# Attention prologue of a fused attention and two-MLP kernel, written in a fixed order

## The chip, the cores and the metric

The kernel runs on one core of a Trainium2 chip. The metric is the device time in microseconds (us). The five engines are called by the names of the profile: PE (TensorE), DVE (VectorE), ACT (ScalarE), POOL (GpSimd) and SP (SyncE, which issues the DMAs here).

## What is computed

```python
def _attn_ref(q, k, v):                      # 8 batches, 8 heads, 576 tokens, 64 wide
    k_p = k.reshape(B, H, Sp, pool, D).mean(axis=3)      # pool = 8, Sp = 72
    v_p = v.reshape(B, H, Sp, pool, D).mean(axis=3)
    scores = scale * np.matmul(q, k_p.transpose(0, 1, 3, 2))
    scores = scores - np.max(scores, axis=-1, keepdims=True)
    attn = np.exp(scores)
    attn = attn / (np.sum(attn, axis=-1, keepdims=True) + 1e-09)
    return np.matmul(attn, v_p)
...
x = attn_out.transpose(0, 2, 1, 3).reshape(4608, 512)
h = x @ w_in;  x = (h - np.tanh(h)) @ w_out      # first MLP, 512 -> 2048 -> 512
h = x @ w_in2; out = (h * np.cos(h)) @ w_out2    # second MLP, the same sizes
```

## The kernel before

The 4608 tokens are cut into nine blocks of 512. A block goes through 16 steps f, one for each 128 of the 2048 hidden columns. In a step PE forms `h` with twelve 512-wide matmuls (`emit_h`, L553: four chunks of x, each as high part times high weight, low part times high weight, high part times low weight), ACT and DVE form h - tanh(h) (`g1_act`, `g1_rest`, `g_second`), and two steps later PE adds the product with `w_out` to four accumulators (`emit_out1`, L590). The second MLP follows for all blocks.

Attention runs beside the first MLP. A batch's K and V are pooled in chunks of 128 pooled rows (`pool_kv`): for batch 0 by one `tensor_reduce` on DVE (L266), for later batches by three additions on POOL (L269 twice, L270). K's sums are copied side by side (L272, ACT), transposed (`kprep`, L302) and put into a block-diagonal tile `bd` by ACT. A Q tile is loaded (`load_q`, SP's queue), transposed (`s1`, L332), multiplied with `bd` in two halves (`s2`, L346; row maximum and subtraction on DVE, L349 and L353; exponential on ACT, L355), normalised (`norm`, L360 to L364), transposed again (`s3`, L375 and L385; copies `ah` and `ar`), and multiplied with V (`pv`, L406; `place_v` puts V's sums into `vbd` and `vbr`). The result is x as a high part `xh` (ACT, L409) and a low part `xl` (DVE, L413). Batch 0 has five tiles: 0 to 3 fill block 0's 512 tokens in two groups of two, tile 4 holds the last 64.

The weights of the first MLP are split into high and low parts in 32 pieces, piece n for step n // 2, w_in before w_out (`converter`): ACT's Prelu into a buffer `cva` (L157), two DVE passes (L166, L168), ACT's copy to the high part (L172), POOL's subtraction to the low part (L162 or L149), one of two buffers held from the first to the last. Pieces for even f stay resident (`wi`, `wo`), those for odd f lie in a ring (`ri`, `ro`).

What stands from L795 to L873 is the prologue: loads, batch 0's attention and the first conversions in program order, which a scheduler turns into an order for each engine; it may also move instructions of block 0 ahead. The steps of block 0 then take attention work of later batches from a list `items`, and conversions by `w1_tick`. Each engine runs its own instructions in its order and waits for the others by semaphores.

Of the kernel before, what the change touches and what calls it, by code (L numbers as in the profile page):

```python
# [8 lines left out]
F32 = mybir.dt.float32  # L9
# [11 lines left out]
T = 0.25  # L21
# [17 lines left out]
def fused_kernel(ctx: ExitStack, tc: tile.TileContext, q, k, v, w1i, w1o, w2i, w2o, out):  # L39
# [98 lines left out]
    def converter(pieces, raws, dest, loaded, done, allowed):  # L138
        prev = None
        a = None  # L140
        for n in range(len(pieces) + 1):
            if n < len(pieces):
# [12 lines left out]
                a = ap.tile([128, 512], F32, tag="cva", name="cva", bufs=2)  # L155
# [99 lines left out]
    def pool_kv(which, b, c):  # L255
# [9 lines left out]
        if b == 0:  # L265
# [5 lines left out]
        if which == "k" and c == NKC - 1:  # L271
            nc.scalar.activation(out=kp[:, :, D:2 * D], in_=kp[:, :, 0:D], func=AF.Copy)  # L272
# [47 lines left out]
    def load_q(t, pool=None, tag="qt", bufs=2):  # L320
        n = t["n"]
        qt = (pool or ap).tile([128, H * D], F32, tag=tag, name="qt", bufs=bufs)
        nc.sync.dma_start(
            out=qt[:n].rearrange("p (h d) -> p h d", h=H),
            in_=q[t["b"], :, t["s"]:t["s"] + n, :].rearrange("h s d -> s h d"))
        t["qt"] = qt
# [9 lines left out]

    def s2(t, half):
        n = t["n"]
        if half == 0:
            t["e"] = eb[t["i"] % 2]  # L340
# [25 lines left out]
    def s3(t, part):  # L366
        n, e, g, o = t["n"], t["e"], t["g"], t["o"]
        if o == 0 and part == 0:
            g["ah"] = ap.tile([128, NP, 320], F32R, tag="ah", name="ah")
            g["al"] = ap.tile([128, NP, 320], F32R, tag="al", name="al")  # L370
            g["ar"] = ap.tile([3 * GR, NG, 320], F32R, tag="ar", name="ar")
        at = att_tile()
        if part == 0:
# [4 lines left out]
            al = g["al"][:, :, o:o + n]  # L378
            if t["b"] in PV32:
                nc.scalar.activation(out=ah.bitcast(F32), in_=av, func=AF.Copy)  # L380
                return None
            nc.scalar.activation(out=ah, in_=av, func=AF.Copy)
# [71 lines left out]
    item(lambda: kprep(0))  # L454
# [206 lines left out]
    w1_conv = converter(w1_pieces, w1_raw, w1_dest, w1_loaded, w1_fin, w1_allowed)  # L661
# [131 lines left out]
    if True:  # L793

        for c in range(3):  # L795
            load_k(0, c)
        load_k(0, 3, cp, "t0", 2)
        load_k(0, 4, cp, "t0", 2)
        load_q(tiles[0])
        w1_load(0)  # L800
        w1_load(1)
        load_q(tiles[1])
        make_identity(nc, ident)
        nc.vector.memset(bias_q, SQ_B)
        nc.vector.memset(bias_m, -T * T)
        nc.vector.memset(bias_r, MAGIC)
        nc.vector.memset(bias_c, HALF_PI)
        nc.gpsimd.memset(kp, 0.0)
        nc.gpsimd.memset(bd, 0.0)
        values()  # L810
        for c, (tag, bufs) in enumerate((("t4", 2), ("t4", 2), ("gh", 3), ("gh", 3), ("gh", 3), ("t2", 1))):
            load_v(0, c, cp, tag, bufs)
        load_q(tiles[2], cp, "xe", 4)
        load_q(tiles[3], cp, "xe", 4)
        load_q(tiles[4], cp, "xe", 4)
        for n in range(2, 6):
            w1_load(n)

# [4 lines left out]
        banks.extend([None, acc[0], "h", acc[1], None, acc[2], "h", acc[3]])  # L823
        for c in range(NKC):
            pool_kv("k", 0, c)
        s1(tiles[0])
        kprep(0)
        kprep(1)
        for c in range(NP + NG):
            pool_kv("v", 0, c)  # L830
        for j, (c0, c1) in enumerate(((0, SP), (SP, 128), (0, SP - RR), (SP - RR, 128))):
            nc.vector.tensor_reduce(mk[:, j:j + 1], ident[:, c0:c1], axis=AX.X, op=ALU.add)
        nc.vector.tensor_reduce(
            mk[:, 4:6], ident.rearrange("p (c g i) -> p g c i", g=2, i=RR), axis=AX.XY, op=ALU.add)
        nc.vector.tensor_scalar(mk, mk, 1.0 / POOL, None, op0=ALU.mult)
        place_v(0)
        for c in range(3):
            load_k(1, c)
        s1(tiles[1])
        l0 = s2(tiles[0], 0)  # L840
        l1 = s2(tiles[0], 1)
        done(l0)
        done(l1)
        w1_tick(2)
        for j in range(n0):
            t = tiles[j]
            if j + 1 < n1:
                l0 = s2(tiles[j + 1], 0)
# [142 lines left out]
```

## Time and profile before

| | us |
|---|---|
| median of three runs | 1785.73 (1785.09 to 1785.97) |
| the profiled execution | 1787.28 |
| its span, first to last instruction | 1785.5 |
| PE busy | 1737.2 |
| first matmul of `h`, block 0 | 59.2 |

The page gives busy time by engine over the whole span. The table by stage gives the same for chosen stretches, with PE's granted clock as a share of 2.4 GHz. The chain of waits follows the work that ended last back to what released it, in order of time. A timeline row begins with its start, in us from the span's start, and ends with the idle time ahead of it and what ended that. A group of instructions is given with its mean duration in ns.

### The profile page before, as it was taken

Reading aid. Unit: us, or ns where it says so; the run is one execution under the profiler, and the core shown is the slowest. Engines: PE = TensorE matmul, PEld = TensorE weight load, DVE = VectorE, ACT = ScalarE, POOL = GpSimd, SP = SyncE. Lnnn points to the kernel's source line nnn. Section 1 sums busy time; section 2 is a strip of 40 time slices with the busy share of each in tenths; the row PEclk is TensorE's granted clock in tenths of the full one; section 3 lists DMA queues with packets and bytes.
Section 4 is the critical chain, followed back from the end, with each engine's and each line's share of the span. In section 5 each row is a group of like instructions: output and inputs, shape, how many; then the busy total and the mean of one; then the engine's idle time right before and its main releaser. Section 6 shows DMA issues by size and latency. Waiting matters only on the chain.

```text
span 1785.5 us, 22632 instructions
## 1 busy us (share of the span) xinstructions
PE 1737.2 (97%) x7960; PEld 1426.6 (80%) x7960; DVE 1244.2 (70%) x2109; ACT 1158.1 (65%) x2079; POOL 279.2 (16%) x342
## 2 busy tenths in 40 slices
PE   5989999999999999999999999999999999999999
PEld 3666878888888888888888888888888888888887
DVE  8699778778888887776666566565656666566655
ACT  4576767767677776766665666666666666666665
POOL 3764244213424141100000000000000000000000
PEclk8799999999999999999999999999999999999999
DMA  7565655645655554523277401010101010101000
GB/s 234 162 215 192 211 161 182 212 159 185 205 177 184 188 197 142 175 100 109 83 262 254 154 0 48 1 48 1 48 1 47 1 47 1 48 1 48 1 24 24
DMA packets 116402, 202.29 MB, mean 113 GB/s; under 512 B 45376, under 2 KB 61760, under 8 KB 116288
## 3 DMA queue, kind: packets, MB, share of 16 engines
q1 hardware_dynamic: 116288, 200.84, 33.9%
q8 instruction: 63, 1.03, 0.2%
q14 instruction: 51, 0.42, 0.1%
HBM read 156.76 MB, written 44.04 MB: 112 GB/s over the span
## 4 chain that ended last, share of the span: by engine, by line
PE 86%; DVE 5%; DMA 3%; ACT 2%; POOL 2%; issue 1%; SPq 0%; POOLq 0%; DVEq 0%; ACTq 0%
PE h L751 22%; PE acc L779 21%; PE h L553 19%; PE acc L590 18%; PE att L406 2%; PE att L346 2%; DMA kv<-in_k_dram 1%; POOL kv L269 1%; PE att L375 1%; DVE cva L168 1%; DMA raw<-in_moe_w_in_dram 1%; DVE gl L583 1%; DVE w L576 1%; PE att L332 1%; DVE w L575 1%
## 5 line engine op out<-in xcount | busy, mean ns | idle before, releaser
L751 PE MATMUL h<-xh,wi 128*128 128x512 f32 x1008 | 330.8, 389 | 0.0
L779 PE MATMUL acc<-wo,gh 128*128 128x512 f32 x1008 | 310.3, 389 | 0.0
L762 DVE SCALAR_TENSOR_TENSOR r<-kk,h 128x512 f32<-128x512 f32 (+1 forms) x145 | 99.1, 684 | 182.2 <-ACT kk L760 181.8
L751 PEld LDWEIGHTS h<-xh,wi 128*128 128x128 f32 x1008 | 189.3, 188 | 39.4
L779 PEld LDWEIGHTS acc<-wo,gh 128*128 128x128 f32 x1008 | 189.2, 188 | 39.3
L770 ACT ACTIVATE r<-r 128x512 f32<-128x512 f32 (+1 forms) x145 | 91.3, 630 | 195.2 <-DVE r L764 195.2
L553 PE MATMUL h<-xh,wi 128*128 128x512 f32 x576 | 199.8, 407 | 1.2 <-POOL wi L162 0.6
L553 PE MATMUL h<-xh,ri 128*128 128x512 f32 x576 | 196.2, 400 | 0.0
L571 DVE SCALAR_TENSOR_TENSOR w<-u,h 128x512 f32<-128x512 f32 x144 | 98.2, 682 | 140.6 <-ACT th L565 140.5
L751 PE MATMUL h<-xl,wi 128*128 128x512 f32 x504 | 196.1, 389 | 0.0
L779 PE MATMUL acc<-wo,gl 128*128 128x512 f32 x504 | 196.1, 389 | 0.0
L772 DVE TENSOR_TENSOR co<-co,h 128x512 f32<-128x512 f32 (+1 forms) x145 | 99.1, 684 | 117.6 <-ACT co L771 117.6
L590 PE MATMUL acc<-gh,wo 128*128 128x512 f32 x576 | 178.9, 392 | 0.0
L590 PE MATMUL acc<-gh,ro 128*128 128x512 f32 x576 | 177.4, 389 | 0.0
L759 ACT ACTIVATE kk<-h,bias_r 128x512 f32<-128x512 f32 (+1 forms) x145 | 99.6, 687 | 91.6 <-PE h L751 91.6
L564 ACT ACTIVATE u<-h 128x512 f32<-128x512 f32 x144 | 85.6, 594 | 91.6 <-PE h L553 91.1
L582 ACT ACTIVATE gh<-w 128x512 fp32r<-128x512 f32 x144 | 90.9, 631 | 66.3 <-DVE w L576 65.2
L583 DVE TENSOR_TENSOR gl<-w,gh 128x512 fp32r<-128x512 f32 x144 | 109.7, 762 | 28.2 <-ACT gh L582 26.0
L553 PEld LDWEIGHTS h<-xh,wi 128*128 128x128 f32 x576 | 109.7, 191 | 24.4 <-POOL wi L162 1.1
L590 PEld LDWEIGHTS acc<-gh,wo 128*128 128x128 f32 x576 | 109.1, 190 | 22.9
L576 DVE COPY_PREDICATED w<-u,th 128x512 f32<-128x512 uint32 x144 | 113.3, 787 | 19.1 <-ACT u L574 6.1
L590 PEld LDWEIGHTS acc<-gh,ro 128*128 128x128 f32 x576 | 108.1, 188 | 22.5
(165 smaller groups left out, 3530.4 us busy)
## 6 DMA issues: line engine op xcount, KB each, us to landing
ri<-s1i SPq DMA_DIRECT2D x64, 512.0 KB, 3.5
ro<-s1o SPq DMA_DIRECT2D x64, 512.0 KB, 3.4
raw<-in_moe_w_in_dram SPq DMA_DIRECT2D x32, 512.0 KB, 3.9
raw<-in_moe_w_out_dram SPq DMA_DIRECT2D x32, 512.0 KB, 4.0
x1s<-xe SPq DMA_DIRECT2D x36, 256.0 KB, 4.7
xr<-x1s SPq DMA_DIRECT2D x36, 256.0 KB, 3.9
out_dram<-xe SPq DMA_DIRECT2D x36, 256.0 KB, 2.1
kv<-in_k_dram SPq DMA_DIRECT2D x32, 256.0 KB, 3.9
```

The costliest lines, as they stand in the source:

```text
L553: nc.tensor.matmul(out=h[:, off:off + m], lhsT=wi[:, c, wsel, :], rhs=xt[:, r:r + m], start=(n == 0), stop=(n == 3 * KC - 1))
L571: nc.vector.scalar_tensor_tensor(w, u, C2, h, op0=ALU.mult, op1=ALU.mult)
L576: step_end[0] = nc.vector.copy_predicated(w, u.bitcast(U32), th)
L582: nc.scalar.activation(out=gh[:, a:e], in_=w[:, a:e], func=AF.Copy)
L583: nc.vector.tensor_tensor(gl[:, a:e], w[:, a:e], gh[:, a:e].bitcast(F32), op=ALU.subtract)
L590: nc.tensor.matmul(out=acc[d], lhsT=wo[:, wsel, d * 128:(d + 1) * 128], rhs=gt, start=(f == 0 and n == 0), stop=(f == NF - 1 and n == 2))
L751: nc.tensor.matmul(out=h, lhsT=wi[:, c, wsel, :], rhs=xt[:, o:o + BLK], start=(n == 0), stop=(n == 3 * KC - 1))
L759: nc.scalar.activation(out=kk[:, a:e], in_=h[:, a:e], func=AF.Identity, bias=bias_r, scale=INV_2PI)
L762: nc.vector.scalar_tensor_tensor(r[:, a:e], kk[:, a:e], -PI2_HI, h[:, a:e], op0=ALU.mult, op1=ALU.add)
L770: nc.scalar.activation(out=r[:, a:e], in_=r[:, a:e], func=AF.Abs)
L772: nc.vector.tensor_tensor(co[:, a:e], co[:, a:e], h[:, a:e], op=ALU.mult)
L779: nc.tensor.matmul(out=acc[t], lhsT=gt[:, t * 128:(t + 1) * 128], rhs=wo[:, wsel, :], start=(f == 0 and n == 0), stop=(f == NF - 1 and n = ...
```

## The change

The prologue is written under `manual_schedule`, which keeps the order of its instructions; the scheduler can still place others between them. In it:
- A one-element exponential comes first on ACT, and with it the table load.
- Q tiles 0 to 3 are loaded from ACT's queue, tile 4 is left to `items`.
- Batch 0's K is copied and transposed in two parts, as its chunks come; its V is summed on POOL.
- The conversion has four buffers instead of two: `wide`, which has the place of `al` (batches 0 and 1 don't use `al`), holds two more.
- Tiles 2 and 3 have score buffers of their own, in the place of resident weights that come later.
- `spin(n)` puts n transposes of the identity into PE's order, 38 in all, into an accumulator that nobody reads.
- The pooling of the next batch's K, tile 4's scores and exponentials move to `items`, and of the conversions 8 calls of `w1_tick` stay where up to 26 were.

```diff
-                a = ap.tile([128, 512], F32, tag="cva", name="cva", bufs=2)
+                a = own[n % len(own)] if own else ap.tile([128, 512], F32, tag="cva", name="cva", bufs=2)
...
-        if b == 0:
+        if b == 0 and which == "k":
             nc.vector.tensor_reduce(o, t[:n].rearrange("p (r d) -> p d r", r=POOL), axis=AX.X, op=ALU.add)
         else:
...
-        if which == "k" and c == NKC - 1:
-            nc.scalar.activation(out=kp[:, :, D:2 * D], in_=kp[:, :, 0:D], func=AF.Copy)
+        if which == "k" and (c == NKC - 1 or (b == 0 and c == KSPLIT[0][1] - 1)):
+            c0 = (KSPLIT[1][0] if c == NKC - 1 else 0) if b == 0 else 0
+            nc.scalar.activation(out=kp[:, c0:c + 1, D:2 * D], in_=kp[:, c0:c + 1, 0:D], func=AF.Copy)
...
     t = tiles[n0]
-    item(lambda: kprep(0))
+    item(lambda t=t: s1(t), lambda t=t: load_q(t))
+    post_kv("k", 1, 0)
+    item(lambda t=t: s2(t, 0), apart=True)
+    post_kv("k", 1, 1)
+    item(lambda t=t: s2(t, 1))
+    post_kv("k", 1, 2)
...
+    post_kv("k", 1, 4)
+    item(lambda: kprep(0), apart=True)
     post(lambda t=t: norm(t))
...
+        with tc.manual_schedule():
+            warm = cp.tile([128, 1], F32, name="warm")
...
+            nc.scalar.activation(out=warm, in_=bias_m, func=AF.Exp)
+            make_identity(nc, ident)
+            for c in range(3):
+                load_k(0, c)
+            load_k(0, 3, cp, "t0", 2)
+            load_k(0, 4, cp, "t0", 2)
+            load_q(tiles[0], queue=nc.scalar)
+            load_q(tiles[1], queue=nc.scalar)
+            w1_load(0)
+            for c, (tag, bufs) in enumerate((("t4", 2), ("t4", 2), ("gh", 3), ("gh", 3), ("gh", 3), ("t2", 1))):
+                load_v(0, c, cp, tag, bufs)
+            load_q(tiles[2], cp, "xe", 4, nc.scalar)
+            load_q(tiles[3], cp, "xe", 4, nc.scalar)
+            for n in range(1, 6):
+                w1_load(n)
...
+            words1.extend(ap.tile([128, 512], F32, tag="cva", name="cva", bufs=2) for _ in range(2))
+            wide = ap.tile([128, 4, 320], F32, tag="al", name="wide").rearrange("p c n -> p (c n)")
+            words1.extend(wide[:, m * 512:(m + 1) * 512] for m in range(2))
...
+            for c in range(KSPLIT[0][1]):
+                pool_kv("k", 0, c)
+            s1(tiles[0])
+            kprep(0)
+            for c in range(KSPLIT[1][0], NKC):
+                pool_kv("k", 0, c)
+            s1(tiles[1])
+            kprep(1)
+            for c in range(NP + NG):
+                pool_kv("v", 0, c)
...
+            def spin(n):
+                for _ in range(n):
+                    nc.tensor.transpose(idle[:, 0:128], ident, ident)
...
+            scored(0)
+            w1_tick(1)
+            exps(0)
+            scored(1)
+            s1(tiles[2])
+            exps(1)
+            w1_tick(1)
+            s1(tiles[3])
+            scored(2)
+            norm(tiles[0])
+            done(s3(tiles[0], 0))
+            done(s3(tiles[0], 1))
+            spin(4)
...
+            spin(8)
+            xs = [pv(tiles[3]["g"], p) for p in range(NP)]
+            for fn in xs:
+                fn()
+            spin(12)
             w1_tick(2)
```

ACT at the start. Before, its order began with the table load behind DVE's K sums (`kp` holds them), then the copy of all five chunks, the first conversion step and the first Q tile's copy:

```order
L272 ACT_TABLE_LOAD [waits DVE_49]
L272 ACTIVATE kp_149<-kp_149 128x5x64 [waits Pool_49]
L157 ACTIVATE cva_283<-raw_168 128x512 [waits DMAHW6_49]
L334 ACTIVATE qT_225<-att_220 128x512 [waits PE_49]
L309 ACTIVATE bd_153<-acc0_82 64x3x72 [waits PE_49,Pool_49]
```

In the changed kernel ACT begins so (`qt` are Q tiles 0 to 3 as loaded):

```order
L821 ACT_TABLE_LOAD
L821 ACTIVATE warm_158<-bias_m_71 128x1 [waits DVE_49]
L326 DMA qt_178<-in_q_dram 128x8x64
L326 DMA qt_180<-in_q_dram 128x8x64
L326 DMA qt_196<-in_q_dram 128x8x64 [waits DMAHW0_49]
L326 DMA qt_198<-in_q_dram 128x8x64 [waits DMAHW3_49]
L275 ACTIVATE kp_149<-kp_149 128x3x64 [waits DVE_49,Pool_49]
L337 ACTIVATE qT_236<-att_231 128x512 [waits PE_49]
```

The table load now waits for nothing, four DMA issues stand ahead of the first K copy, and the fourth waits on the semaphore of the first Q tile's landing.

POOL between its memsets and the low half of f=1's first weights (`ri`). Before (`wi`, `wo` are f=0's, `ro` is f=1's second; `kv` are chunks of the next batch's K):

```order
L162 TENSOR_TENSOR wi_307<-cva_283,wi_307 128x4x128 [waits Activation_49]
L162 TENSOR_TENSOR wo_308<-cva_310,wo_308 128x512 [waits Activation_49]
L162 TENSOR_TENSOR ri_375<-cva_355,ri_375 128x4x128 [waits DMAHW2_49,Activation_49]
L269 TENSOR_TENSOR kv_257<-kv_257 128x256 [waits DMAHW6_49]
L269 TENSOR_TENSOR kv_257<-kv_257 128x128 [waits Pool_49]
L270 TENSOR_TENSOR kp_149<-kv_257 128x64 [waits PE_49,Pool_49]
L162 TENSOR_TENSOR ro_391<-cva_377,ro_391 128x512 [waits DMAHW3_49,Activation_49]
```

In the changed kernel six chunks of V come first, then `ro` of f=1, five chunks of the next K, six of the next V, with `wi` of f=0, `wi` of f=2 and `wo` of f=0 between; then these rows (`kv_1901` to `kv_1912` are chunks of the batch after that, `wo_606` is f=2's, `ri_526` f=1's):

```order
L271 TENSOR_TENSOR kv_645<-kv_645 32x128 [waits Pool_49]
L271 TENSOR_TENSOR kv_1901<-kv_1901 128x256 [waits DMAHW4_49]
L272 TENSOR_TENSOR vr_151<-kv_645 32x64 [waits Pool_49]
L271 TENSOR_TENSOR kv_1901<-kv_1901 128x128 [waits Pool_49]
L271 TENSOR_TENSOR kv_1903<-kv_1903 128x256 [waits DMAHW5_49]
L271 TENSOR_TENSOR kv_1903<-kv_1903 128x128 [waits Pool_49]
L164 TENSOR_TENSOR wo_606<-cva_219,wo_606 128x512 [waits Activation_49]
L271 TENSOR_TENSOR kv_1910<-kv_1910 128x256 [waits DMAHW7_49]
L271 TENSOR_TENSOR kv_1910<-kv_1910 128x128 [waits Pool_49]
L271 TENSOR_TENSOR kv_1912<-kv_1912 128x256 [waits DMAHW0_49]
L271 TENSOR_TENSOR kv_1912<-kv_1912 128x128 [waits Pool_49]
L164 TENSOR_TENSOR ri_526<-wide_220,ri_526 128x4x128 [waits Activation_49]
```

`ri` of f=1 has moved from POOL's third row of work to behind 17 chunks, the first two additions ("heads") of four later chunks, and five other conversions.

PE around the `h` of f=1. Before it ran without a wait for POOL of its own, behind transposes of tile 4 and of the next Q tile:

```order
L385 MATMUL att_595<-ident_69,eb0_154 32x64 [waits Activation_49]
L385 MATMUL att_595<-ident_69,eb0_154 32x64
L332 MATMUL att_602<-ident_69,qt_529 128x128 [waits DMAHW1_49,PE_49,Activation_49]
L332 MATMUL att_602<-ident_69,qt_529 128x128 x3
L553 MATMUL h_619<-xh0_74,ri_375 128x512
L553 MATMUL h_619<-xl0_78,ri_375 128x512
L553 MATMUL h_619<-xh0_74,ri_375 128x512
```

Now tile 4's scores stand there, and the third matmul waits for POOL:

```order
L351 MATMUL att_567<-bd_153,qT_520 64x144 [waits Activation_49]
L351 MATMUL att_567<-bd_153,qT_520 64x144
L351 MATMUL att_579<-bd_153,qT_520 64x144 [waits PE_49]
L351 MATMUL att_579<-bd_153,qT_520 64x144
L569 MATMUL h_611<-xh0_74,ri_526 128x512 [waits Activation_49]
L569 MATMUL h_611<-xl0_78,ri_526 128x512
L569 MATMUL h_611<-xh0_74,ri_526 128x512 [waits Pool_49]
```

The third matmul of f=1 now depends on the last of the POOL rows above; tile 4's transposes and the next Q tile's have moved behind it.

## Rows read from the trace of the kernel before

**Rows 1.** Page, busy us by engine (share of the span) and instructions.

```profile
PE 1737.2 (97%) x7960; PEld 1426.6 (80%) x7960; DVE 1244.2 (70%) x2109; ACT 1158.1 (65%) x2079; POOL 279.2 (16%) x342
```

**Rows 2.** Stages: stretch, length, busy by engine, granted clock, DMA share, GB/s.

```profile
0.00:59.20 59.20, 33.93 (x125) 22.97 (x125) 44.23 (x85) 26.62 (x62) 29.46 (x43) 0.79 0.64 195
...
47.60:59.20 11.60, 11.27 (x26) 5.55 (x26) 5.42 (x10) 4.00 (x11) 10.63 (x18) 0.50 0.24 64
...
59.20:168.00 108.80, 96.27 (x422) 73.59 (x421) 93.65 (x144) 74.58 (x151) 65.79 (x75) 0.94 0.63 208
168.00:200.00 32.00, 32.00 (x149) 25.52 (x148) 26.70 (x44) 23.94 (x46) 6.37 (x5) 1.00 0.62 196
```

**Rows 3.** Chain of waits from 0 to 60 us: start, us, what.

```profile
9.62 1.28 ACT L272
...
18.99 1.89 DVE va L266 x2
...
45.20 1.72 POOL wo L149
46.94 0.67 ACT cva L157
```

**Rows 4.** Timeline of PE, prologue and the first two steps.

```profile
13.22 1.30 PE L346 MATMUL att<-bd,qT 128*128 128x144 f32 x4 [0.37 <-ACT bd L309]
...
47.67 1.09 PE L375 MATMUL acc<-ident,eb 128*128 128x128 f32 x4 [8.55 <-ACT cva L157]
48.55 0.64 PE L385 MATMUL att<-ident,eb 128*32 128x128 f32 x2
...
66.95 0.62 PE L553 MATMUL h<-xh,ri 128*128 128x512 f32 x2
67.41 0.39 PE L553 MATMUL h<-xl,ri 128*128 128x512 f32 x1
```

**Rows 5.** SP's queue (timeline), then DMA issues of 0 to 60 us, us to landing.

```profile
5.97 3.87 SPq L246 DMA_DIRECT2D kv<-in_v_dram  x4
...
raw<-in_moe_w_out_dram SPq DMA_DIRECT2D x5, 512.0 KB, 6.4
...
kv<-in_v_dram SPq DMA_DIRECT2D x8, 256.0 KB, 4.6
qt<-in_q_dram SPq DMA_DIRECT2D x5, 256.0 KB, 5.7
```

**Rows 6.** POOL's groups by form, 53 to 64 us, DVE nearly idle: busy us, mean ns.

```profile
L269 POOL TENSOR_TENSOR kv<-kv 128x256 f32<-128x256 f32 x4 | 2.9, 721 | 0.0
L269 POOL TENSOR_TENSOR kv<-kv 128x128 f32<-128x128 f32 x4 | 1.8, 452 | 0.3
...
L270 POOL TENSOR_TENSOR va<-kv 128x64 f32<-128x64 f32 x4 | 1.3, 318 | 0.3
L162 POOL TENSOR_TENSOR ro<-cva,ro 128x512 fp32r<-128x512 f32 x1 | 1.3, 1270 | 0.0
```

**Rows 7.** The same, 32 to 53 us, DVE busy.

```profile
L269 POOL TENSOR_TENSOR kv<-kv 128x256 f32<-128x256 f32 x4 | 4.6, 1150 | 0.0
...
L269 POOL TENSOR_TENSOR kv<-kv 128x128 f32<-128x128 f32 x4 | 2.5, 632 | 0.2
L270 POOL TENSOR_TENSOR kp<-kv 128x64 f32<-128x64 f32 x4 | 2.2, 561 | 0.2
```

**Rows 8.** DVE: one timeline row, then groups by form of 20 to 53 us.

```profile
26.17 0.74 DVE L364 TENSOR_TENSOR eb<-eb,sm 128x576 f32<-128x576 f32 x1
...
L364 DVE TENSOR_TENSOR eb<-eb,sm 128x576 f32<-128x576 f32 x4 | 4.8, 1194 | 0.0
...
L353 DVE TENSOR_TENSOR eb<-acc,mx 64x288 f32<-64x288 f32 x1 | 0.4, 441 | 0.0
```

**Rows 9.** DVE's groups by form, 60 to 170 us.

```profile
L575 DVE SCALAR_TENSOR_TENSOR w<-s,w 128x512 f32<-128x512 f32 x13 | 15.3, 1179 | 0.0
...
L571 DVE SCALAR_TENSOR_TENSOR w<-u,h 128x512 f32<-128x512 f32 x13 | 8.8, 676 | 4.7 <-ACT th L565 4.7
```

## What I predict

> **What bounds the kernel now.** The page first: PE is busy 97% of the span [rows 1], so time can only come from stretches where PE waits or runs slowly. The table by stage shows where they are [rows 2]. From 168 us PE is full (32.00 of 32.00). Before block 0's first `h` at 59.2 it is busy 33.9 of 59.2 us, and between 59.2 and 168 it lacks 108.8 - 96.3 = 12.5 us. In its last part, 47.6 to 59.2, the granted clock is 0.50, the 1.2 GHz level: a busy PE at half speed. So the prologue holds some 25 us of idle PE and some 6 us lost to the clock, and block 0 another 12 us.
>
> The chain of waits tells who holds the prologue [rows 3]. It starts with K: the ACT table load (1.28) stands on it because ACT loads its table only after the K sums. Then DVE sums V between the score halves (three rows like the one shown, 5.6 us). Later POOL's subtractions of the weight conversion hold it, and ACT's first conversion step waits for a POOL that still reads one of two buffers (45.20, then ACT at 46.94). Only then do the last transposes run: PE had been idle 8.55 us [rows 4], the clock was down, and the 11.5 us to the first `h` followed.
>
> So the change is worth what moves in PE's order up to block 0's second step (f=1). From block 1's first step on, PE's instructions stand in the same order in both programs; what counts is when block 0 gets going and how freely it runs. I compare one point, the third matmul of `h` for f=1, which needs the low half of f=1's weights from POOL. Before it ran at 66.95 [rows 4].
>
> **The change part by part.**
>
> *Start: table load, ACT queue.* The warm activation takes the load of 1.28 us off the chain, and the copy of the first three K chunks goes out without waiting for the last two. Against it, ACT now issues four Q loads, and the fourth waits for the first Q tile's landing ahead of ACT's first K copy (order below). A Q load took 5.7 us to land [rows 5]; issued after the table load, near 2.5, it lands near 8, before the K sums end. ACT was idle there, so the issues cost nothing; if Q lands later, ACT's K copy and everything behind it slip by as much. I take the first scores 1 us earlier than 13.22 [rows 4], with bounds of 0 and 2.
>
> *DVE.* V's six sums leave: three rows of 1.9, 5.7 us. The scores and normalisation of tile 4 go to block 0: four passes at 0.44, 1.05 and some 1.3 for the small ones [rows 8], 4 us. DVE was busy 44.2 us before 59.2 [rows 2], so 34.5 remain, of which 6 precede the first scores. From 13 on that makes 41.5, plus some 4 us of waiting (for Q tile 2, and for the fourth weight load, which now stands ahead of the later score passes): 46. The last `xl` that the first `h` needs stands three conversions earlier, near 42. So the `h` of f=0 can be done at 46 to 47 with a full clock. With the clock down as in 47.6 to 59.2, the last transposes and products take 11.5 again instead of half that, and it ends near 55. Before: 65.5. The identity transposes lie in PE's waits and cost nothing as long as DVE is late; after the last products 12 of them stand ahead of the first `h`, at most 12 x 0.22 (four transposes took 0.88 from 47.67 on at the low clock) = 2.6 us.
>
> *POOL, the term that decides.* All of V's sums now go through it, and the scheduler puts the weights of f=1 far behind. Before, they were POOL's third piece of work after the memsets; now they follow 17 pooled chunks (6 of V and 5 of K, 6 of the next V), four heads of later chunks and five other conversions (order below). A chunk costs 721 + 452 + 318 ns = 1.49 us while DVE is nearly idle [rows 6], but 1150 + 632 + 561 = 2.34 while DVE works [rows 7]; a head 1.17 or 1.78, a conversion 1.27 [rows 6].
> - V lands from about 10 on (issued from 5.97 before, 4.6 us to land [rows 5]; now a little earlier in SP's row, but beside Q). Six chunks end near 20.
> - Then POOL stands: the next conversion needs the fourth weight load, which SP issues near 12.5 (an estimate: V's second chunk must have landed first; before, it such loads went out from 16.79 on). At 6.4 us [rows 5] it lands near 19; ACT, DVE, ACT follow, so POOL resumes near 23.3 and is done with it at 24.6.
> - Left are 11 chunks, 4 heads and 5 conversions. Quiet: 16.4 + 4.7 + 6.4 = 27.5, to 52. Contended throughout: 25.7 + 7.1 + 6.4 = 39.2, to 64. DVE has its own list until about 46, so most of it is contended: one conversion and about 8.6 chunks by 46, then 13.4 quiet, to 59. DVE's two-input work is thinner per us than in the stretch of rows 7, so I take 58.
>
> PE is ready at 47 to 55 and so waits for POOL at f=1, whatever the transposes do to the clock. That wait takes the place of the one removed.
>
> The rows show the two engines in each other's way: DVE's normalising product took 0.74 at 26.17, and 1.19 in the mean over 20 to 53 [rows 8]. The Trainium skill's page "SBUF — State Buffer", section "SBUF: two separate sides", says why: GpSimd and a DVE instruction with two SBUF inputs share one port pair, and the loser blocks for a whole instruction. The rows agree in kind. Its page "GPSIMD Engine Reference", section "4.1 Engine selection", would also keep a sum along the free dimension on VectorE; here 0.95 us on DVE stands against 1.49 to 2.34 on POOL.
>
> *From there on.* At 58 PE has waited and I count the clock as down: the ten matmuls left of f=1, 0.23 each at the full clock (66.95 to 67.41 for two [rows 4]), cost 2.3 more. Fifteen small transposes that before had been done by 66.95 (K and the next Q, tile 4's) are still to do: 15 x 0.11 = 1.7. Gain: 66.95 - 58 - 2.3 - 1.7 = 5.0 us.
>
> *Block 0.* DVE's 512-wide passes there are stretched too (the third pass of the activation 1179 ns [rows 9], against 0.68 for its neighbours of the same shape). Four heads, some 5 us of POOL, are already done, and four instead of two conversion buffers loosen the ring of ACT, DVE and POOL. Of PE's 12.5 us of gaps I give back 1.5, with bounds of 0 and 3.
>
> Sum: 5.0 + 1.5 = 6.5 us. The profiled execution has a span of 1785.5 and 1.8 us around it (1787.28); the median is 1785.73. So the span becomes 1779.0 and the median **1779.2**.
>
> **The rivals.**
> 1. *PE is the bound at f=1, not POOL.* If POOL runs at its quiet prices (ends at 52) and the identity transposes hold the clock, 66.95 - 52 - 1.7 = 13.3, with block 0's bound 16: 1770 to 1775. For it: POOL's quiet rows. Against it: DVE works all through this stretch. 20%.
> 2. *The gain is handed back at POOL: no change.* Contended throughout, POOL ends at 64: 66.95 - 64 - 2.3 - 1.7 = -1, and +1.5: 1785 to 1786. The same comes out, a little better, by strict exclusion: quiet POOL from 24.6 to 52 and the two-input DVE work of that time (some 9 us) end at 61, a gain of 2.0 + 1.5: 1782. That is what the "SBUF — State Buffer" rule gives by itself. For it: rows 7. Against it: DVE's list ends before POOL's. 21%.
> 3. *Slower.* One mechanism: the fourth weight load lands late. SP's loads of V and weights each wait for an earlier landing on the same semaphore, Q's small pieces run beside them, and every later POOL instruction stands behind that one conversion. Each us later than 19 moves f=1 by one. With contended prices it is slower by 3.6 us once POOL ends past 68, that is, with a landing near 23: about 1790. For it: four loads stand between. Against it: the same loads landed in 6 us before. 11%.
> 4. *The fixed order doesn't do what it says.* If the clock stays down, f=0 ends at 55, still ahead of POOL's 58: inside the forecast.
>
> **How the numbers follow.** The forecast (POOL last at f=1, a gain of 3.6 to 10, so 1776 to 1782) 48%, rival 1 20%, rival 2 21%, rival 3 11%. Faster by over 0.2% (3.6 us; about what a measurement of this kernel can tell): 48 + 20 = 68%. Same 21%, slower 11%. The range runs from rival 1's far end, 1770, to 1788, which leaves out most of rival 3 and a little of rival 1.
>
> **What would show it.** The table load before 3 us and the first scores near 12. DVE with no V sums. POOL nearly full from 23 to the low half of f=1's weights, ending at 55 to 61, with `h` of f=1 waiting for POOL there and the clock down. Block 1's first step earlier by 5 to 8 us, and equal distances from there on. It is wrong if `h` of f=1 waits for something else (DVE or a load), if POOL's chunks cost 1.5 us beside a busy DVE, or if block 0 itself becomes longer or shorter by more than 3 us.

## The result: 21 us slower, almost all of it far behind the place that was changed

The changed kernel takes 1806.6 us (1805.58 to 1810.46), the kernel before 1785.67: a ratio of 1.0122, interval 1.0104 to 1.0139. The forecast was 1779.2, with a range of 1770 to 1788. The profiled execution took 1810.46 us, with a span of 1808.4 against 1785.5.

The page of the kernel after, busy us by engine, against [rows 1]:

```profile
PE 1765.8 (98%) x7998; PEld 1431.2 (79%) x7998; DVE 1240.9 (69%) x2103; ACT 1160.8 (64%) x2081; POOL 290.5 (16%) x360
```

PE is busy 28.6 us longer, with only 38 instructions more (the transposes of the identity). A prologue that waits longer would show idle time; here the matmuls themselves take longer. The stages of the kernel after (stretch, length, busy by engine, granted clock, DMA share, GB/s), the first three against [rows 2]:

```profile
0.00:55.60 55.60, 37.16 (x151) 26.68 (x151) 34.39 (x66) 23.65 (x57) 39.12 (x70) 0.82 0.72 215
44.40:55.60 11.20, 11.20 (x59) 8.16 (x58) 5.54 (x10) 6.68 (x15) 8.37 (x14) 0.85 0.42 141
...
168.00:200.00 32.00, 30.49 (x138) 23.79 (x139) 24.94 (x42) 22.73 (x45) 5.41 (x5) 1.00 0.58 192
...
1080.00:1280.00 200.00, 200.00 (x867) 162.49 (x866) 120.22 (x196) 122.77 (x195) 0.00 (x0) 1.00 0.07 23
```

and the same 200 us of the kernel before:

```profile
1080.00:1280.00 200.00, 200.00 (x884) 165.62 (x883) 121.47 (x198) 125.50 (x199) 0.00 (x0) 1.00 0.09 32
```

In both, PE is full and the granted clock is 1.00, yet 867 matmuls fit where 884 did: 230.7 ns each in place of 226.2. That is 2% in a stretch in which no instruction was changed.

Where the time arises, read from the start of `h` in each step (first line: us in the kernel before; then each kernel's difference to it; minus is earlier):

```
                     f=0    f=1    f=4    f=11   f=15   block 1  block 4  block 9  last h
before               59.20  66.41  84.03 148.74 178.59   184.50   501.16   992.24  1772.65
after                -3.59  -6.67  -3.59  -5.01  -2.98    +0.52    +2.40    +7.68   +23.0
e4 (old distance)    -4.55  -7.69  -4.53  -5.62  -3.53    +0.03    -0.18    +0.57    +0.6
e17 (old distance)   -6.22  -9.32  -6.21  -7.57  -5.50    -1.96    -3.21    -2.53    -2.5
```

There are two separate findings. The prologue's lead was there, 6.67 us at the second step, and block 0 took it back. And from block 1 on the kernel lost 22 us more: some 7 in the rest of the first MLP, where PE still waits now and then, and 15.3 in the second MLP, 1.7 us in each of its nine blocks.

Up to f=1 the times came near the forecast, in part by other ways than it named. PE of the kernel after (timeline), against [rows 4]:

```profile
12.10 1.33 PE L351 MATMUL att<-bd,qT 128*128 128x144 f32 x4
...
35.19 1.19 PE L412 MATMUL att<-ah,vbd 128*128 128x256 f32 x2 [3.50 <-POOL kp L272]
...
48.84 0.60 PE L412 MATMUL acc<-ah,vbd 128*128 128x256 f32 x2
...
55.60 0.50 PE L569 MATMUL h<-xh,wi 128*128 128x512 f32 x1
...
60.65 0.73 PE L569 MATMUL h<-xh,ri 128*128 128x512 f32 x2 [0.18 <-POOL ri L164]
```

and POOL's timeline, against [rows 6, 7]:

```profile
12.34 1.26 POOL L271 TENSOR_TENSOR kv<-kv 128x256 f32<-128x256 f32 x2 [8.59 <-DMA kv<-in_v_dram]
13.67 0.32 POOL L272 TENSOR_TENSOR va<-kv 128x64 f32<-128x64 f32 x1
...
24.95 1.44 POOL L164 TENSOR_TENSOR ro<-wide,ro 128x512 fp32r<-128x512 f32 x1 [2.25 <-ACT ro L174]
...
59.33 1.27 POOL L164 TENSOR_TENSOR ri<-wide,ri 128x512 fp32r<-128x512 f32 x1
```

### The profile page after: what moved, and what is told of

Same layout as the page of the kernel before. It is cut to its first block, busy times and chain, and to the rows that moved or that the text cites. A ratio compares the mean times of both kernels' runs of the same rounds, so it can differ in the third digit from the quotient of the medians.

```text
span 1808.4 us, 22714 instructions
## 1 busy us (share of the span) xinstructions
PE 1765.8 (98%) x7998; PEld 1431.2 (79%) x7998; DVE 1240.9 (69%) x2103; ACT 1160.8 (64%) x2081; POOL 290.5 (16%) x360
## 4 chain that ended last, share of the span: by engine, by line
PE 86%; DVE 5%; DMA 3%; POOL 3%; issue 2%; ACT 2%; SPq 0%; POOLq 0%; DVEq 0%; ACTq 0%
PE h L767 22%; PE acc L795 22%; PE h L569 18%; PE acc L606 18%; PE att L412 2%; PE att L351 2%; POOL kv L271 1%; DMA kv<-in_k_dram 1%; PE att L381 1%; DVE w L591 1%; DMA raw<-in_moe_w_out_dram 1%; DVE w L592 1%; DMA qt<-in_q_dram 1%; DVE w L587 1%; PE att L335 0%
## 5 line engine op out<-in xcount | busy, mean ns | idle before, releaser
L767 PE MATMUL h<-xh,wi 128*128 128x512 f32 x1008 | 337.5, 396 | 0.0
L569 PE MATMUL h<-xh,wi 128*128 128x512 f32 x576 | 199.6, 407 | 6.6 <-ACT wi L174 2.9
L271 POOL TENSOR_TENSOR kv<-kv 128x256 f32<-128x256 f32 (+7 forms) x166 | 118.6, 718 | 80.8 <-DMA kv<-in_v_dram 42.7
L569 PEld LDWEIGHTS h<-xh,ri 128*128 128x128 f32 x576 | 108.4, 189 | 27.1 <-POOL ri L164 3.4
L592 DVE COPY_PREDICATED w<-u,th 128x512 f32<-128x512 uint32 x144 | 114.8, 798 | 20.1 <-ACT u L590 7.6
```

What stands on the lines that cost most here:

```text
L271: nc.gpsimd.tensor_tensor(t[:n, :w], t[:n, :w], t[:n, w:2 * w], op=ALU.add)
L569: nc.tensor.matmul(out=h[:, off:off + m], lhsT=wi[:, c, wsel, :], rhs=xt[:, r:r + m], start=(n == 0), stop=(n == 3 * KC - 1))
L592: step_end[0] = nc.vector.copy_predicated(w, u.bitcast(U32), th)
L767: nc.tensor.matmul(out=h, lhsT=wi[:, c, wsel, :], rhs=xt[:, o:o + BLK], start=(n == 0), stop=(n == 3 * KC - 1))
```

## Experiments on the late 22 us

The change adds one tile in the middle of SBUF: `warm`, 4 bytes a partition, behind `xh` and `xl` and ahead of everything else. In the built program it takes 32 bytes there, so all weights, `gh`, `gl` and the attention's tiles start 32 bytes later: `xh0` at 1792 as before, the first weights at 75552 instead of 75520. The order of PE's late instructions is the same. So the first theory was the addresses; the rival, something that the new prologue starts (clock, queues).

**e1: `warm` 64 bytes wide.** All starts are multiples of 64 again.

```diff
-            warm = cp.tile([128, 1], F32, name="warm")
+            warm = cp.tile([128, 16], F32, name="warm")
```

> The changed kernel with one number different: the tile `warm`, which the change adds for an early table load, is 64 bytes a partition wide instead of 4, so that every tile behind it (the MLP's weights wi, wo and its gh, gl) starts at a multiple of 64 bytes again, as before the change; the order of the instructions is the same. Theory (the addresses): the matmuls of the second MLP go back from 233.4 ns (h) and 228.8 ns (acc) a piece to 226.7, the 22.5 us that arose between block 1 and the end are gone, and the time is 1779 to 1786 us; where in that range says what the prologue itself is worth. Rival (something that the new prologue starts, and not the addresses): nothing moves, 1806.6 us and 233.4 ns.

Measured 1808.64 us, ratio 1.0138 (1.0108 to 1.0167): nothing gained, and `h` at 233.3 ns, as the rival said. As I had put it, multiples of 64, the theory fell.

**e2: the kernel before with an unused tile of 4 bytes** behind `xl`. Nothing else differs.

```diff
+    cp.tile([128, 1], F32, name="pad")
     acc = [ps.tile([128, BLK], F32, name=f"acc{c}") for c in range(4)]
```

> The kernel before with an unused tile of 4 bytes a partition between xl and the tiles behind it, so that the weights and gh, gl start 32 bytes past a multiple of 64; nothing is computed or ordered otherwise. Theory (the addresses): 233 ns (h) and 229 ns (acc) a matmul in the second MLP, 1806 to 1810 us. Rival (the new prologue does it): 226.7 ns and 1785.7 us, as before.

1805.97 us, 1.0116 (1.0095 to 1.0137). The rival is out: the old program, with the same order of instructions on every engine, is as slow with one unused tile. The cause is an address; what about it, the next runs tell.

**e3: one such tile ahead of `xh`, one behind `xl`.** Now `xh` and `xl` move by 32 bytes and the rest by 64.

> The kernel before with two unused tiles of 4 bytes, one ahead of xh and one behind xl: xh and xl, which the first product of the MLP streams, start 32 bytes past a multiple of 64, while weights and gh, gl stay at multiples of 64. If it is the mismatch between weights and streamed data that costs: h at about 233 ns, acc at 226.7, some 3456 x 6.7 ns x the part of it that runs without waits, 1797 to 1805 us. If it is the weights' own start alone: 226.7 ns everywhere, 1785.7 us. If any start off 64 bytes costs its own time: h slower than 226.7 as well.

1806.09 us, 1.0114 (1.0084 to 1.0145). `h` came at 233.4 ns, as the mismatch said, but `acc` at 228.9 where I had 226.7, and the time lies above the 1797 to 1805 that went with it.

**e4: the changed kernel with `warm` ahead of `xh`.** Everything moves by 32 bytes.

> The changed kernel with its 4-byte tile ahead of xh instead of behind xl: xh, xl, the weights and gh, gl all start 32 bytes past a multiple of 64. If the mismatch costs: 226.7 ns for h and acc, 1779 to 1786 us. If each start off 64 bytes costs by itself: h at 233 ns or more, acc at 229 ns, 1806 us or more.

1788.69 us, 1.0020 (1.0007 to 1.0033): 226.7 ns as forecast, the time 2.7 us above the forecast's upper end. So no start counts by itself. What counts is the distance between `xh`, `xl` and what lies behind them: +32 (e2, e3, after) and +64 (e1) cost the full price, +0 nothing.

**e5, e6, e13: the kernel before with 256, 512 and 128 bytes** in place of the 4.

> The kernel before with an unused tile of 256 bytes a partition between xl and the tiles behind it (before: wi starts 73728 bytes, 36 x 2048, behind xh0). So far a change of that distance by 32 or by 64 bytes cost 6.7 ns of each h matmul, and shifting both sides alike cost nothing. If the distance counts only up to some multiple of 256 or less: 226.7 ns, 1785.5 us. If it has to be a multiple of more: about 233 ns for h and 1803 to 1809 us.

> The same with 512 bytes, the length of the row of weights that one matmul loads in a partition (128 x 4 bytes). If distances count modulo that length or less: 226.7 ns and 1785.5 us; if modulo more (2048 is the length of the row streamed): about 233 ns for h and 1803 to 1809 us.

> The kernel before with an unused tile of 128 bytes a partition between xl and the tiles behind it. 32 and 64 bytes cost 6.7 ns of each h matmul, 256 and 512 next to nothing. If the distance counts modulo 128: about 226.7 ns and 1784 to 1787 us. If modulo 256: 230 to 234 ns for h and 1796 to 1809 us.

One timed run each: 1786.1 us with 256, 1786.4 with 512, 1804.39 with 128. The distance counts modulo 256, as far as six distances (0, 32, 64, 128, 256, 512) tell.

**e17: the changed kernel with `warm` 256 bytes wide**, one number different from the kernel that was measured.

```diff
-            warm = cp.tile([128, 1], F32, name="warm")
+            warm = cp.tile([128, 64], F32, name="warm")
```

> The changed kernel with one number different: `warm` is 256 bytes a partition wide instead of 4, so that the distance from xh to the weights grows by 256 bytes instead of 32. By the runs so far the distance counts modulo 256 and nothing else of the late 22 us is left: 226.7 ns for h and acc, 1784 to 1790 us, the prologue's lead gone at block 1 as in the fourth run. If it is the equal start of both sides that counted there: 233 ns and 1806 us.

1786.47 us, 1.0011 (1.0002 to 1.0020). This one number is worth 20.1 us of the 20.9 by which the changed kernel was slower.

The rows behind these verdicts: matmuls of PE by form from 1100 to 1600 us (busy us, mean ns of one), first e2, slow:

```profile
L752 PE MATMUL h<-xh,wi 128*128 128x512 f32 x640 | 214.3, 396 | 0.0
L780 PE MATMUL acc<-wo,gh 128*128 128x512 f32 x640 | 198.8, 392 | 0.0
```

then e17, fast:

```profile
L767 PE MATMUL h<-xh,wi 128*128 128x512 f32 x640 | 210.0, 389 | 0.0
L795 PE MATMUL acc<-wo,gh 128*128 128x512 f32 x648 | 199.5, 389 | 0.0
```

Taken from start to start of two of the same kind in that stretch, a matmul takes (mean):

```
distance modulo 256         h, ns    acc, ns
  0 (before, e4, e5, e6, e17)  226.7   226.7
 32 (after, e2, e3)            233.4   228.9
 64 (e1)                       233.3   228.5
128 (e13)                      232.9   228.0
```

A block of the second MLP has 192 matmuls of each kind: 192 x 6.7 + 192 x 2.2 ns make the 1.7 us a block. In the first MLP (200 to 960 us) the same pitch of `h` is 229.2 ns in the kernel before and 233.0 in the kernel after. So part of the price is paid there at distance 0 too, and a block lost only 0.9 us; what causes that part is open.

The timeline of the kernel before shows what happens at once in that stretch. While one matmul streams `xh`, the weights of the next are loaded (PE, then PE's load unit):

```profile
1400.24 0.39 PE L751 MATMUL h<-xh,wi 128*128 128x512 f32 x1
```

```profile
1400.24 0.19 PEld L751 LDWEIGHTS h<-xl,wi 128*128 128x128 f32 x1
```

Both reads start together. That they get into each other's way at certain distances would fit the pitch of `h`, but this is argued: no row shows the two reads, and no run moved the weights apart from `gh`, `gl` and the rest. Another engine's accesses are the rival. GpSimd does nothing in that stretch; and in e1 two `h` matmuls are 233.4 ns apart while VectorE is idle and ScalarE busy, and 233.3 the other way round, so neither of these two is needed for the price. It also leaves open why the first five matmuls of `acc` behind an `h` are slow as well (230, 236, 228, 232, 231 ns, then 227), in the kernel after, although `wo` and `gh` keep their distance in all runs. The Trainium skill's page "SBUF — State Buffer", section "SBUF: two separate sides", says that PE never waits on anyone for SBUF. The runs differ by 6.7 ns a matmul with addresses alone, and the measurement decides.

## Experiments on the lead that block 0 took back

Block 0, from the first `h` to block 1, lasted 125.3 us before and 129.4 after. Engines in it, before and after (columns as above):

```profile
59.20:184.50 125.30, 112.77 (x494) 86.14 (x493) 109.14 (x167) 87.33 (x175) 71.00 (x79) 0.95 0.64 211
```

```profile
55.60:185.00 129.40, 115.24 (x505) 86.54 (x504) 117.08 (x181) 92.64 (x184) 73.47 (x69) 0.96 0.62 204
```

VectorE is busy 8 us more there. Eight weight pieces were converted ahead of the first `h` before, four now; and tile 4's scores and normalisation have moved in. What PE waits for changed sides. The waits of the kernel before in that stretch (us in total, times, longest):

```profile
PE att L375 <- DVE eb L353: 5.7, 2, 3.8
PE att L406 <- DVE xl L413: 2.3, 1, 2.3
...
PE h L553 <- POOL wi L162: 0.6, 1, 0.6
PE h L553 <- ACT wi L172: 0.6, 1, 0.6
```

and of the kernel after:

```profile
PE h L569 <- ACT wi L174: 2.9, 2, 1.7
...
PE h L569 <- POOL wi L164: 2.5, 2, 1.9
...
PE h L569 <- POOL ri L164: 1.5, 3, 0.7
```

Weights cost 1.2 us of waits before and 6.9 now: the steps have caught up with the conversion. But other waits went, and waiting is the smaller part of what block 0 took back. From the first `h` of f=1 to block 1, before and after:

```profile
66.41:184.50 118.09, 105.56 (x471) 81.27 (x470) 107.63 (x164) 84.48 (x167) 66.53 (x69) 0.97 0.63 207
```

```profile
59.73:185.03 125.30, 111.14 (x485) 83.47 (x484) 113.73 (x177) 90.84 (x181) 69.50 (x64) 0.96 0.63 209
```

Of the 7.2 us that this stretch is longer, 1.6 are idle time of PE (14.2 in place of 12.5) and 5.6 are PE's own busy time: some 15 more transposes, and the same 180 `h` matmuls at 49.1 us in place of 45.6 (48.9 in e4). Some twenty of its 512-wide matmuls follow each other at over 400 ns, the pitch of the low clock, and ten of the kernel before's. With the old distance (e4) it is the same: 14.7 us idle, 111.1 busy.

How far one execution can be read, the runs on the addresses tell, since they change no order. The order of the kernel before (before, e2, e3, e5, e6, e13) reached block 1 at 180.8 to 185.5 us, with a block 0 of 122.2 to 126.7 us; the new order (after, e1, e4, e17) at 182.5 to 185.0, with 129.4 to 130.0. So block 0 did become longer and the lead is gone at block 1, but a difference of less than 5 us at block 1 between two executions shows little.

The theory was that VectorE's work paces block 0, with the rival that another engine or the attention's chains do. All kernels below are e4, unless the text says otherwise; the scheduler orders block 0 anew in each, so none differs from e4 by its edit alone.

**e7 and e8: the second operation of a conversion left out, or done twice, in pieces 8 to 15.** The edit of e7; e8 repeats the line for the same pieces.

```diff
+                if not own or not 8 <= n < 16:
                     nc.vector.scalar_tensor_tensor(au, lo, 29, au, op0=ALU.logical_shift_right, op1=ALU.bitwise_or)
```

> The changed kernel with its 4-byte tile ahead of xh (as in the fourth run, whose block 0 lasts from 54.65 to 184.53 us with VectorE busy 128.8 of 129.9 us), without VectorE's second operation of a weight conversion in pieces 8 to 15, which all fall into block 0 (0.85 us each in the kernel of that run; the weights lose their last three bits there). Theory (VectorE bounds block 0, and what the prologue put off onto it ate the lead): block 1 starts 5 to 7 us earlier, at 178 to 180, and the time is 1780 to 1784 us. Rival (ScalarE, GpSimd or the order of PE's work bounds block 0): under 2 us earlier.

> The same kernel with that operation run twice in pieces 8 to 15 (the second time gives the same bits): 6.8 us more of VectorE in block 0. Theory (VectorE bounds block 0): block 1 starts 5 to 8 us later, at 190 to 192, and the time is 1794 to 1797 us. Rival (another engine or the order bounds it): under 2 us later.

The theory missed in both. (VectorE was busy 117.2 of e4's 129.9 us, not 128.8 as I had written.) e8 reached block 1 at 185.85, 1.3 later than e4, as its rival said (1787.07 us, 1.0016). But it is no test: the eight added operations took 5.7 us, others became shorter, and VectorE was busy 116.9 us in block 0, no more than in e4. e7, with 5.7 us less of VectorE in block 0, was 8 us ahead of e4 at f=11 and then 3.6 behind it at block 1 (188.14; 1790.78 us, 1.0027). Its PE between the two points:

```profile
142.29 1.22 PE L414 MATMUL att<-ah,vbd 128*128 128x256 f32 x2 [5.12 <-DVE xl L421]
143.45 1.21 PE L414 MATMUL att<-ar,vbr 32*128 32x256 f32 x2
```

The last products of the attention waited for a VectorE queue that had other work ahead of them; the granted clock was 0.50 from 140 to 150, and a pair that elsewhere takes 0.70 took 1.22. So less work on VectorE alone doesn't make block 0 shorter.

**e14 and e15: both of VectorE's operations left out in pieces 8 to 31**, in the kernel before and in e4.

> The kernel before without VectorE's two operations of a weight conversion in pieces 8 to 31 (the weights of those pieces are wrong then; their loads, ScalarE's and GpSimd's parts stay). It takes some 36 us of VectorE's busy time out of block 0. If the conversion of the pieces paces block 0: block 0 (first `h` to block 1's first step) at 95 to 112 us instead of 125.3. If the attention's and the MLP's own chains do: 118 to 126 us.

> The same left out of the kernel of the fourth run (the change, with weights and xh at the old distance), whose block 0 takes 129.9 us. Theory (what the prologue puts off and VectorE's share in the conversion eat the lead in block 0): with that work gone the lead at block 1 over the fourteenth run is 3 to 8 us, about what it is at the first steps. Rival (the order of the attention's work in block 0 eats it): the lead is again gone at block 1, within 2 us.

Their block 0:

```profile
59.00:182.40 123.40, 113.64 (x495) 88.44 (x493) 76.99 (x119) 89.16 (x176) 68.97 (x79) 0.91 0.67 218
```

```profile
56.50:176.70 120.20, 113.54 (x506) 87.51 (x504) 85.19 (x132) 91.63 (x184) 65.94 (x69) 0.94 0.68 220
```

With 32 us of VectorE's work gone, the block of the kernel before is only 1.9 us shorter, inside the spread of its order: there the theory falls, and its end is held by something else. The changed kernel's block is 9.7 us shorter than e4's, far outside the spread of the new order, and at block 1 it is 5.7 us ahead of e14, nearly its 6.3 at f=1. In the changed kernel, then, the conversion's VectorE work does stand between the lead and block 1, as far as one execution each can tell. Of the 5.7, 2.8 are left at the end (1778.72 against 1781.49 us, one timed run each): blocks 3 to 6 took the rest.

**e9 and e12: V's sums on VectorE in e4; V's sums on GpSimd in the kernel before.**

> The changed kernel with its 4-byte tile ahead of xh (the fourth run), and with the sums over V back on VectorE (6 instructions of about 1 us, in place of 18 on GpSimd that took some 12 us). If the sums on GpSimd were a gain of the prologue: first `h` later than that run's 54.65 us by 2 to 6 us, and the steps behind it too. If GpSimd is what the first steps wait for, and VectorE has the room: first `h` at 50 to 54 us and the second step's third matmul 2 to 6 us earlier. Either way, if block 0 hands back what it is given (as the fourth, seventh and eighth runs suggest): block 1 at 183 to 187 us and 1785 to 1789 us in all.

> The kernel before with one part of the change alone: the sums over V on GpSimd. VectorE loses about 6 us of its list ahead of the first `h`, GpSimd gains some 12. If that part is worth something by itself: first `h` at 55 to 58 us instead of 59.2. If GpSimd's low halves of the first weights come late by it: first `h` or the second step's third matmul 1 to 8 us later than 59.2 and 66.95. Block 1 within 2 us of 184.5 if block 0 hands back what it is given.

e9: first `h` at 58.73, 4.1 later than in e4, and block 1 at 190.77, not at 183 to 187 (1793.86 us, 1.0050). e12: first `h` at 65.22, 6.0 later than before, as PE's last transposes start 6.0 later and wait longer, against [rows 4]:

```profile
53.69 1.09 PE L375 MATMUL acc<-ident,eb 128*128 128x128 f32 x4 [11.51 <-ACT cva L157]
```

and block 1 5.7 later, where I had at most 2 (1790.35 us, 1.0026). At the first `h` the same move is worth 4 us in the new order and costs 6 in the old one, where GpSimd's conversions stand behind it: the sixth ended at 52.93 in e12 and at 46.91 before. In e12 block 0, which takes leads back, didn't make good a delay.

**e10: no identity transposes.**

> The kernel of the fourth run without the 38 transposes of the identity that fill TensorE's waits in the prologue. If they hold the clock up: granted clock 0.5 in the second group of pv and in the first step, first `h` at 56 to 60 us in place of 54.65, and the lead over the kernel before at the second step 2 to 5 us smaller than 7.7. If they don't: within 1 us of that run at each step.

First `h` at 54.03 and the start of f=1 8.3 us ahead (54.65 and 7.7 with them), and the second group of pv ran at full speed:

```profile
48.62 0.70 PE L413 MATMUL acc<-ah,vbd 128*128 128x256 f32 x2 [0.32 <-ACT ah L386]
```

So the transposes did nothing up to the first `h`; the rows don't show them holding a clock that falls without them. At f=2 e10 was 2.1 us behind e4, more than the 1 us that I had allowed: PE waited 2.83 us for GpSimd's low half of f=1, and 0.24 in e4. The 11 us that this run lost between f=3 and f=4 (1795.01 us, 1.0068) come with another order of GpSimd's queue, in which K sums of the next batch stand ahead of f=3's weights (PE waits 4.96 us for `ri` at 78.29); these losses say nothing on the transposes.

**e11: tile 4's scores back in the prologue.**

> The kernel of the fourth run with the scores of tile 4 (its transposes, its two halves of scores with maxima, subtractions and exponentials) back in the prologue, behind tile 3's last transposes, as the kernel before has them; they no longer stand in block 0. If what the prologue put off is what ate the lead in block 0: first `h` later by at most 2 us, block 1 at 180 to 183 us instead of 184.5, 1782 to 1785 us in all. If block 0 is held by something that doesn't shrink with it: block 1 at 184 to 186 us.

Missed: first `h` at 60.80, 6.2 later than e4, and block 1 at 192.5 (1793.18 us, 1.0042). It put its work ahead of the last pv on three engines, so it doesn't tell what tile 4 costs in block 0.

**e16 and e18: three more weight pieces asked for ahead of the first `h`**, in e4 and in e17.

```diff
             spin(12)
-            w1_tick(2)
+            w1_tick(14)
```

> The kernel of the fourth run with three more weight pieces converted behind the last pv of the prologue, so that 8 pieces are asked for ahead of the first `h`, as in the kernel before, and not 5. If it is the lead of the conversion over the steps that is missing in block 0: the 32nd piece ends 3 to 7 us before the fourth run's 178, block 1 starts at 178 to 182 us, 1780 to 1784 us in all. If not: block 1 at 184 to 187, as before.

> The same with the three weight pieces asked for ahead of the first `h`, as in the sixteenth run: the best that these runs point to. If that run's lead at block 1 (4.6 us, of which 3.0 were left at the end) is real: 1780 to 1784 us, 0.1 to 0.3 per cent below the kernel before. If it was chance: within 0.1 per cent of the seventeenth run.

First `h` came at 45.0 and 44.4, some ten us before e4's. The first pv group started 7.1 us earlier than in e4 (28.15 against 35.25) and ran at the full clock; PE had waited 3.4 us for VectorE's normalising product (6.5 in e4) and 1.35 for GpSimd (3.9). At f=1 PE then waited for the low half, which GpSimd reached only six us earlier (52.40, and 58.37 in e4), and the clock was down behind that wait (e16):

```profile
28.15 0.67 PE L413 MATMUL att<-ah,vbd 128*128 128x256 f32 x2 [1.35 <-POOL kv L272]
...
53.71 1.22 PE L570 MATMUL h<-xh,ri 128*128 128x512 f32 x2 [3.90 <-POOL ri L165]
```

```profile
52.40 1.26 POOL L165 TENSOR_TENSOR ri<-wide,ri 128x512 fp32r<-128x512 f32 x1
```

The edit didn't give the conversion a lead, so it doesn't test one: one piece was through GpSimd at the first `h`, four in e4; the eighth ended at 73.4 us, 63.9 in e4; and the 32nd at 176 and 178, as in e4 (178), not 3 to 7 earlier. Block 0 grew to 134.9 and 136.9 us, and block 1 came at 179.9 and 181.3. e16 took 1785.09 us (1.0002, 0.9984 to 1.0019), e18 1783.57 (0.9991, 0.9980 to 1.0001). That is 2.9 us below e17 (twelve timed runs each, standard error 1.1), as forecast, and the lowest of the kernels that leave no work out; but against the kernel before its interval holds 1. Its profiled execution, 1787.25 us, is one of the slower ones: its 3.2 us at block 1 were gone at the end.

Taken together: first `h` at 44.4, 45.0, 53.0, 54.65, 55.6 and 59.2 (e18, e16, e17, e4, after, before) gives block 1 at 181.3, 179.9, 182.5, 184.5, 185.0 and 184.5. Fifteen us in, five out, and the order of the kernel before alone spreads over 4.7 us there.

## Why the prediction was wrong, by its own steps

The kernel after from 13 us, where the forecast's sum for VectorE starts, to the last `xl` ahead of the first `h` (columns as above; VectorE's is the third busy time):

```profile
13.00:54.83 41.83, 31.94 (x130) 22.80 (x130) 26.26 (x50) 18.17 (x44) 34.54 (x60) 0.76 0.67 211
```

- **The start: right.** The table load runs at 0.73 to 2.01, first scores at 12.10; forecast 1 us ahead of 13.22. PE waited 5.60 us for the first Q tile, ahead of K's sums and so off the path.
- **VectorE and the `h` of f=0: wrong, by VectorE's waiting.** The forecast's 46 to 47 us, or 55 with the clock down, are the end of f=0's `h` (65.5 before). It ended at 58.7, 3.7 us behind the later one. VectorE's work was as forecast, 34.4 us up to the first `h` against 34.5. Its waiting was not: between 13.00 and the last `xl`, which came at 54.83 and not near 42, it was idle 15.6 us where I had some 4. PE in turn waited 6.2 us for VectorE's normalising product and 3.50 for GpSimd ahead of the first pv group, which ran at the low clock (1.22 a pair). Behind it the clock was full, where I had it down.
- **GpSimd as the one that decides at f=1: near in time, hardly so in effect, and in part by luck.** V's six chunks ended at 22.69 (forecast 20), the conversion behind them at 26.39 (24.6), the low half of f=1 at 60.60 (58), and PE's third matmul came at 60.65. But PE was there only 0.18 us earlier, not at 47 to 55: the two met. A faster GpSimd would have gained nearly nothing there; in e16, with PE ten us earlier, the wait was 3.90. GpSimd's own time is near by two errors that cancel: its additions took 831 and 575 ns in the mean, between my quiet and contended prices, so it worked 30.2 us where I had 33.4, and it waited 2.5 for ScalarE's part of the conversion, where I had nothing.
- **The deductions behind f=1.** I had a net gain of 5.0 us; the lead was 6.3 at the third matmul (66.95 - 60.65) and 6.1 at f=2's start. The 2.3 for the clock weren't due, since it was full. The transposes came later than I had them, between f=2 and f=4: there PE's busy time is 1.6 us longer than before (I had 1.7), it waits 0.9, and the lead falls to 3.6.
- **Block 0 at +1.5, bounds 0 and 3: wrong.** It was -7.2 us in the changed kernel (from 6.67 ahead at f=1 to 0.52 behind at block 1), -7.7 in e4 and -7.4 in e17. I counted the work taken out of VectorE's prologue as gone from the path, and not as what block 0 has to do in its place: 8 us more of VectorE, and a conversion lead of four pieces instead of eight. I also read PE's 12.5 us of gaps as room to give back: they became 14.2, and PE's own work behind f=1 grew by 5.6. e15 shows, in one execution, that the conversion's VectorE work costs the changed kernel its lead. Whether by VectorE's time or by the late pieces isn't separated, since e8 and e16 changed neither as meant; what else holds block 0's end (in the kernel before it hardly moves without the conversion) stays open.
- **"Equal distances from there on": wrong, and the larger error.** The order of PE's late instructions was the same, and I took equal order for equal time. The term that is missing is a 4-byte tile that changes the distance of two operands: 22 us of the 23 between the spans, 20.1 of the medians.
- **The rivals.** The clock at f=1 was up, as in rival 1, but GpSimd ended at 60.6 and not at 52, so its 13.3 us didn't come. Rival 2's end, no change, is what the rest of the change is worth without the distance (e17: 1.0011), but not by its way: GpSimd handed nothing back, block 0 did. Rival 3's load wasn't late enough to matter: GpSimd had its conversion at 24.95, forecast 23.3. The slower result came by none of them. Rival 4 came in part: the clock was down in the first pv group, and f=0 still ended ahead of GpSimd; e10 shows the clock full at the second pv group with and without the transposes.

## What to carry over

A new tile moves the tiles behind it: here one of 4 bytes moved them by 32. In a kernel with PE full, compare the addresses of what the matmuls stream and of their weights before and after; here the three distances that were no multiple of 256 bytes cost 3% of each `h` in the second MLP. A small tile ahead of both (e4) or padded to 256 bytes (e17) cost nothing of that. Count matmuls in a stretch where PE is full: it shows in one row what no wait shows.

Work taken out of a prologue isn't saved by that: here the block behind it, on the same engines, took the lead back. Follow the lead at every step up to where PE is full, and first see how far executions of one order spread there (4.7 us here).

## What the runs showed of the hardware that I had not expected

- In the second MLP PE's 512-wide matmuls took 226.7 ns with xh and the tiles behind it at a distance of 0 modulo 256 bytes, and 232.9 to 233.4 ns for `h` (228.0 to 228.9 for `acc`) at 32, 64 and 128. Granted clock 1.00 in all.
- It depends on the distance, not on either start: with `xh`, `xl` and all tiles behind them moved by 32 bytes together (e4) it was 226.7 ns.
- The clock came back without the transposes put there for it: in e10 the granted clock was 0.54 from 34 to 44 us and 0.91 from 47 to 55, behind 9 us of products that ran without a gap. With the transposes (after) it was 0.50 and 0.96 in the same stretches.
